# Attention and gated MLP on one core: a new order of the same steps from the 200th step on

## The chip, the core and the metric

The kernel runs on one core of one Trainium2 chip. The metric is device time in microseconds (us). A core has five engines with an instruction queue each: PE (TensorE, the matrix unit), DVE (VectorE), ACT (ScalarE), POOL (GpSimd) and SP (SyncE, which here only issues DMAs). Each works its queue strictly in order: an instruction that waits holds up everything behind it on its engine. Engines wait for one another through semaphores.

## The reference

The computation has two parts, all in fp32, and the output of the first is the input of the second:

```python
# attention, B=8 batches, H=8 heads, S=576, D=64, window 128
scores = q @ k.T / 8;  scores += -slope[h] * |i - j|
scores = where(0 <= i - j < 128, scores, -1e9)
attn = softmax(scores)                       # row maximum taken off first
x = (attn @ v) with the heads side by side   # (8, 576, 512)
# gated MLP
u, v = split(gelu_tanh(x @ w_in), 2)         # 512 + 512 columns
v_n = (v - mean(v)) / sqrt(var(v) + 1e-6) * g_ln
v_s = w_sg @ v_n (over the sequence) + b_sg
out = x + (u * v_s) @ w_out
```

## The kernel before, in words

The work is cut into 2015 named steps. A step is a handful of instructions of one engine: one transpose group, one group of exponentials, one DMA issue. The function `attention_gmlp` defines them all and then builds them in the order of one string, `ORDER` (L1150 to L1232). The loop below it (L1234 to L1250) runs the steps in that order and ties every instruction to the one before it on its engine, so the string fixes the queue of each engine word for word. How the steps of different engines mix in the string also decides which on-chip buffer a step gets: pools hand out buffers in the order of the string (2 banks each of the PSUM pools `ps_s`, `ps_a`, `ps_m`, 1 `px`, 2 `qk`), and a step that takes a buffer waits for the last reader of its earlier content.

The 64 (batch, head) problems are 32 *pairs* n (batch n//4, two heads). The steps of pair n, each a letter and n:

- `q`, `L`: loads of q and k (L250) and of v (L257, L259), issued by SP.
- `a`, `c`, or `*` for both: score matmuls on PE (L278). `A` `B` `C` `G`: bias, mask and row minimum of the negated scores on DVE (L302, L295).
- `e` `E` `f` `F` `j`: exponentials on ACT (L311). `R`: inverse of the row sums on DVE (L322, L323). `r` `s` `S`: scaling by it on POOL (L334).
- `t` `T`: transposes of the two heads on PE (L347) into a bank of `ps_a`; `z` the first block's (L360). `X` `Y`: masked copies of them to the one buffer `px` on DVE (L356). `V`: attn @ v on PE (L384, L388), which reads `px`.
- `p` `x` on ACT and `2` on DVE (L396): the result gathered in SBUF. `h` (L401), `l` (L218), `k`: its split in a high and a low part. fp32 products run as three matmuls of such parts, high x high, high x low, low x high (L607 to L609).

The MLP of batch b has, with b as the digit behind the letters: `w` and `v` (x times the columns of v, 512 wide, L607 to L609), `vg` gelu (ACT L786), `n..`/`vn` the normalization (L725 to L742), `tt` `tj` `tg` the last 64 rows (PE L796 and L798, DVE L802 and L803, ACT L811), `u`/`U` the u columns (PE L607 to L609 for batches 0 and 1, L905 for later ones) with their evacuations `uc`, `ue` (DVE L914), `ut`, `y` the product with w_sg (L607 to L609, L940, L941), `gm` the gate (DVE L946), `gh` (ACT L1006) `gl` (POOL L224) `gt` (DVE L1019) its split, `O` the product with w_out (PE L1059), `oa` (DVE L1066, L1069) and `D` the stores (SP L1081). `Us` `Uh` `Ul` (DVE L649 and L659 among them) add rows of weights once, early in the program, and `lu`, `lo` (SP L686) load such sums again per batch. The early steps `i` `d` `b` `o` `+` `H` `-` load and split the weights (ACT L192, L194, L203; DVE L196, L198, L208). `W` steps are filler matmuls (L1139).

ACT needs another function table for gelu than for exp. Where a gelu step follows an exponential in the order, a one-element gelu is put in ahead (L1237), whose row in the trace is preceded by the load of the table; the way back loads one at the exponential (L311).

Of the kernel before, what the change touches and what calls it, by code (L numbers as in the profile page):

```python
# [21 lines left out]
def attention_gmlp(  # L22
# [1123 lines left out]
    for b in range(B):  # L1146
# [10 lines left out]
        l2 v03 v02 v00 v01 W1 e5 j5 vg03 H10 vg02 vg00 vg01 -5 b9 o9 -7 -4 nv30b nv00b nv10b -10 +9 nv00p u000 u030
        u001 F5 k0 H9 nv10c nv00c -9 E5 nv00h f5 k3 nv30c vn00 L5 i11 q7 i8 wl1 q4 tl R5 a4 u031 A4 B4 s5 t5 nv20b r5
        z5 uc00 wH1 k2 tH uc03 j4 E4 w-1 nv10p S5 nv20p t- e4 nv10h X5 c4 C4 f4 G4 P5 F4 bl L4 wl0 tt0 T5 u020 Y5 R4
        vn01 tj0 s4 r4 u021 V5 t4 nv20c u010 tg0 d11 nt0b nv30p x5 p5 wH0 S4 nt0p w-0 X4 25 T4 z4 u011 Y4 nv20h uc02  # L1160
        nv30h P4 bH nt0c vn03 b- vn02 V4 nt0h x4 d8 p4 uc01 tn0 b11 o11 b8 24 o8 y020 y021 *7 +11 ug0 A7 +8 B7 y000
        y001 H11 j7 H8 Us0 C7 G7 -11 -8 Us1 gm02 gm00 F7 E7 f7 e7 q9 q6 L6 *6 A6 R7 gh00 gh02 h4 B6 C6 e6 q8 L7 s7
        y010 y011 t7 S7 gl02 r7 T7 y030 G6 gm01 X7 F6 E6 f6 j6 R6 gl00 s6 S6 Y7 y031 z7 gm03 gh01 h5 P7 V7 p7 gh03
        gl01 t6 T6 X6 Y6 Oa0 x7 gl03 r6 O00 z6 27 oa00 Us2 l4 l5 P6 h7 V6 p6 x6 Us3 26 O01 h6 l6 l7 *8 oa01 A8 B8 C8
        Us4 G8 u100 u101 e8 *9 E8 f8 j8 F8 R8 A9 B9 u110 s8 S8 r8 t8 C9 k4 k7 Uh1 uc10 E9 j9 f9 e9 k5 k6 Ul1 X8 G9
        u111 T8 Y8 Uh0 z8 Ul0 Us5 F9 uc11 P8 tt1 L9 D00 L8 V8 u130 Us6 R9 s9 tj1 Ud1 S9 t9 u120 Uh2 tg1 X9 Us7 Ul2 Ud2
        Ud0 D01 q10 q11 Us8 Us9 nt1b T9 u131 uc13 x8 28 u121 Y9 nt1c O03 nt1p r9 z9 Uh3 nt1h uc12 P9 Ul3 ks0 ks1 ks2
        V9 p9 x9 p8 oa03 ks3 29 ks4 tn1 kh0 kh1 kl0 O02 ks5 *10 A10 B10 C10 G10 j10 e10 E10 f10 F10 oa02 kl1 v10 *11
        v11 A11 R10 vg10 vg11 B11 nv01b nv01c C11 nv11b r10 s10 nv01p S10 nv11p z10 t10 ug1 v12 nv11c X10 v13 T10 P10
        nv11h vn11 nv01h vn10 vg12 nv21b G11 vg13 nv31b Y10 nv21c nv31c ks6 nv21p h9 l9 nv31p ya100 ya110 ya101 ya111  # L1170
        f11 e11 nv21h nv31h j11 kd0 q12 q13 L10 L11 D03 kd1 D02 V10 vn12 kh2 F11 E11 vn13 y100 y101 y110 y111 ks7 kl2
        gm10 ks8 ks9 R11 kh3 gm11 kl3 y120 y121 s11 t11 y130 gh11 gl11 y131 x10 210 gm12 gt11 p10 h8 gh15 X11 gm13 O11
        S11 gl15 r11 gt12 T11 z11 O15 h10 gh12 gh16 gh13 P11 Y11 oa11 gl12 V11 x11 p11 gl16 gt13 O16 211 gh17 oa15
        oa16 gt14 *13 gl13 O13 gl17 ut25 oa13 O17 A13 oa17 O12 B13 oa12 h11 gh14 gl14 l8 O14 C13 oa14 G13 l10 l11 E13
        k10 uh25 k9 k11 k8 v20 v21 vg20 ul25 vg21 j13 ut26 ut27 nv02b nv02c nv02p nv02h nv12b nv12p nv12c nv12h vn20
        vn21 *12 tt2 U21 kd2 lu21 lu22 q14 lu20 L12 D11 D10 q15 L13 tj2 U25 uh27 f13 uh26 e13 ue21 A12 B12 ut24 ul27
        ul26 U26 F13 ue25 U23 uh24 E12 ue26 U27 C12 ue23 G12 R13 e12 f12 j12 F12 U22 ue27 R12 ul24 U24 ue22 r12 s12
        z12 t12 S12 tg2 nt2b nt2p s13 X12 nt2c ue24 v22 T12 Y12 v23 vg22 nv22b P12 nt2h tn2 vg23 V12 p12 x12 nv32b
        nv32c 212 nv22c nv22p nv32p S13 h12 l12 r13 ug2 nv22h nv32h ya200 ya210 *14 A14 B14 vn22 ya201 t13 ya211 z13
        vn23 y200 y201 X13 gm20 C14 y210 y211 y220 T13 gm21 G14 E14 P13 f14 gh21 j14 F14 e14 Y13 gl21 y221 *15 y230  # L1180
        R14 A15 gt21 B15 gm22 C15 r14 s14 S14 y231 gh25 f15 gm23 gl25 gt23 gt22 z14 t14 V13 E15 gh23 P14 p13 x13 gh27
        O21 gh22 j15 X14 213 lo21 q16 lo22 D13 q17 D12 lo20 L14 L15 T14 O25 G15 Y14 gh26 V14 p14 F15 x14 e15 gl23 gl27
        gl22 oa21 gl26 O26 oa25 O23 ut35 gt24 214 R15 oa26 oa23 *16 A16 B16 C16 O27 s15 S15 r15 z15 t15 h14 k12 gh24
        h13 E16 P15 j16 l13 gl24 l14 G16 oa27 X15 k13 e16 uh35 F16 f16 O22 T15 Y15 O24 *17 R16 oa22 oa24 A17 B17 V15
        s16 r16 S16 x15 p15 215 h15 ul35 l15 C17 f17 e17 t16 X16 T16 G17 ut37 Y16 L16 q19 lu32 D21 lu30 D23 L17 q18
        lu31 D20 v30 z16 k15 k14 j17 P16 F17 E17 tt3 tj3 *18 V16 R17 ut36 tg3 vg30 nt3b nt3c nt3p uh37 x16 ul37 nt3h
        v31 216 nv03b tn3 U31 uh36 vg31 ue31 U35 A18 B18 nv13b ut34 ul36 U36 r17 s17 t17 z17 ue35 uh34 ue36 C18 nv13c
        U33 ue33 X17 S17 nv03p nv13p ul34 U37 U32 ue37 T17 U34 nv13h P17 j18 E18 f18 vn31 ue32 G18 nv03c Y17 nv03h
        ue34 p16 F18 e18 vn30 v33 D22 R18 *19 vg33 V17 x17 ug3 A19 s18 B19 C19 nv33b 217 nv33c v32 t18 ya310 vg32 E19
        nv23b nv23c r18 S18 nv33p nv23p j19 ya300 ya301 z18 ya311 X18 nv23h nv33h p17 vn32 vn33 e19 h17 G19 h16 P18  # L1190
        F19 l17 k17 f19 lo32 L19 L18 lo31 q20 q21 lo30 T18 y310 Y18 y300 y301 *20 gm30 R19 A20 V18 B20 x18 r19 s19 S19
# [79 lines left out]
```

## Time and profile before

| what | value |
|---|---|
| median of 3 runs | 577.96 us (577.95 to 578.33) |
| span of the profiled execution | 577.4 us |
| PE busy | 560.8 us, 97% of the span |
| DVE busy | 473.8 us, 82% |
| ACT busy | 378.6 us, 66% |
| POOL busy | 308.0 us, 53% |
| DMA | 69.78 MB, mean 121 GB/s |

The profiled execution's span is 577.4 us, about half a microsecond under the median of the runs; what the runs count beyond it lies around the span. Busy time is a sum over the whole program; where an engine waits, and for which other, is read from single stretches.

### The profile page before, as it was taken

Reading aid. Unit: us, or ns where it says so; the run is one execution under the profiler, and the core shown is the slowest. Engines: PE = TensorE matmul, PEld = TensorE weight load, DVE = VectorE, ACT = ScalarE, POOL = GpSimd, SP = SyncE. Lnnn points to the kernel's source line nnn. Section 1 sums busy time; section 2 is a strip of 40 time slices with the busy share of each in tenths; the row PEclk is TensorE's granted clock in tenths of the full one; section 3 lists DMA queues with packets and bytes.
Section 4 is the critical chain, followed back from the end, with each engine's and each line's share of the span. In section 5 each row is a group of like instructions: output and inputs, shape, how many; then the busy total and the mean of one; then the engine's idle time right before and its main releaser. Section 6 shows DMA issues by size and latency. Waiting matters only on the chain.

```text
span 577.4 us, 14654 instructions
## 1 busy us (share of the span) xinstructions
PE 560.8 (97%) x5495; PEld 512.7 (89%) x5495; DVE 473.8 (82%) x1324; ACT 378.6 (66%) x1063; POOL 308.0 (53%) x365
## 2 busy tenths in 40 slices
PE   5889999999999999999999999999999999999997
PEld 4667899998899799997999998998989999998997
DVE  7989998799989868899788987878897988666646
ACT  7988997466853867467776576746695667833422
POOL 3676646530436543575447753496347653576325
PEclk9989999999999999999999999999999999999999
DMA  8675213216403413454260465135332606012502
GB/s 297 190 235 199 72 45 121 69 46 243 167 37 125 156 37 99 146 192 129 60 212 10 140 204 173 43 103 168 130 120 65 214 2 197 2 35 96 171 1 82
DMA packets 43561, 69.78 MB, mean 121 GB/s; under 512 B 3554, under 2 KB 31202, under 8 KB 43492
## 3 DMA queue, kind: packets, MB, share of 16 engines
q1 hardware_dynamic: 43492, 68.86, 36.7%
q8 instruction: 43, 0.70, 0.5%
q14 instruction: 26, 0.21, 0.1%
...
## 4 chain that ended last, share of the span: by engine, by line
PE 90%; DVE 5%; DMA 2%; ACT 1%; issue 1%; POOL 0%; SPq 0%; DVEq 0%; ACTq 0%
PE ps_m L607 13%; PE ps_m L1059 13%; PE ps_m L609 12%; PE ps_m L608 12%; PE ps_m L905 12%; PE ps_a L347 5%; PE ps_s L384 4%; PE ps_s L278 4%; PE ps_a L278 4%; PE ps_m L384 3%; DMA qk<-qkT 2%; PE ps_m L941 2%; PE ps_m L940 1%; DVE px L356 1%; DVE e L295 1%; PE ps_m L796 1%
## 5 line engine op out<-in xcount | busy, mean ns | idle before, releaser
L334 POOL TENSOR_TENSOR e<-e,rr 128x256 f32<-128x256 f32 (+2 forms) x116 | 80.7, 718 | 97.0 <-DVE rr L323 84.9
L311 ACT ACTIVATE e<-e,stats 128x128 f32<-128x128 f32 (+1 forms) x288 | 110.6, 386 | 17.7 <-DVE stats L295 17.1
L224 POOL TENSOR_TENSOR region<-u,region 128x288 fp32r<-128x288 f32 (+1 forms) x78 | 77.7, 1016 | 44.7 <-ACT region L1006 16.2
L356 DVE TENSOR_TENSOR px<-ps_a,m_both 128x1024 f32<-128x1024 f32 x64 | 77.4, 1216 | 5.9 <-PE ps_a L347 5.4
L607 PE MATMUL ps_m<-ws,region 128*128 128x288 f32 x256 | 78.2, 306 | 0.0
L609 PE MATMUL ps_m<-ws,region 128*128 128x288 f32 x256 | 75.7, 296 | 0.0
L608 PE MATMUL ps_m<-ws,region 128*128 128x288 f32 x256 | 75.6, 295 | 0.0
L730 POOL TENSOR_TENSOR rs<-rs,mhalf 128x1 f32<-128x1 f32 (+1 forms) x40 | 30.2, 756 | 57.4 <-DVE rs L727 57.2
L218 POOL TENSOR_TENSOR xs<-xf,xs 128x288 fp32r<-128x288 f32 (+1 forms) x48 | 49.9, 1060 | 13.8 <-ACT xs L401 13.8
L311 ACT ACTIVATION_READ_ACCUMULATOR e<-e,stats 128x1 f32 x288 | 54.4, 189 | 0.0
L1006 ACT ACTIVATE region<-u 128x576 fp32r<-128x576 f32 x35 | 23.7, 684 | 43.4 <-PE ps_m L608 17.4
L607 PEld LDWEIGHTS ps_m<-ws,region 128*128 128x128 f32 x256 | 48.3, 189 | 1.5 <-issue 0.8
L608 PEld LDWEIGHTS ps_m<-ws,region 128*128 128x128 f32 x256 | 48.2, 188 | 0.1
L609 PEld LDWEIGHTS ps_m<-ws,region 128*128 128x128 f32 x256 | 48.1, 188 | 0.1
L607 PE MATMUL ps_m<-wi,xs 128*128 128x512 f32 x112 | 46.9, 418 | 0.1
L1066 DVE TENSOR_TENSOR xf<-ps_m,xf 128x576 f32<-128x576 f32 x48 | 35.7, 750 | 10.9 <-PE ps_m L1059 10.1
L609 PE MATMUL ps_m<-wi,xs 128*128 128x512 f32 x112 | 44.3, 395 | 0.0
L608 PE MATMUL ps_m<-wi,xs 128*128 128x512 f32 x112 | 44.2, 395 | 0.0
L946 DVE TENSOR_TENSOR u<-ps_m,u 128x576 f32<-128x576 f32 x32 | 24.0, 752 | 18.7 <-PE ps_m L941 11.5
L347 PE MATMUL ps_a<-ident,e 128*128 128x128 f32 x256 | 38.0, 275 | 1.0 <-DVE px L356 1.0
L295 DVE CUSTOM_DVE_ANT_0 e<-ps_s,bias 128x128 f32<-128x128 f32 (+1 forms) x140 | 34.9, 287 | 2.5
L278 PE MATMUL ps_s<-qk 64*64 64x192 f32 (+2 forms) x576 | 31.5, 333 | 5.3 <-DMA qk<-qkT 4.9
(217 smaller groups left out, 1600.9 us busy)
## 6 DMA issues: line engine op xcount, KB each, us to landing
...
```

The lines of the kernel that those rows point to most:

```text
L218: (engine or nc.gpsimd).tensor_tensor(out[:, cs], a[:, cs], b[:, cs], op)
L224: nc.gpsimd.tensor_tensor(out[:, fs], a[:, fs], b[:, fs], ALU.subtract)
L278: return lambda: nc.tensor.matmul(banks[half][to, c:c + k1 - k0], qk[js, 0, q0:q0 + R], qk[js, 1, k0:k1], start=True, stop=True)
L311: nc.scalar.activation(x, x, AF.Exp, bias=self.nm[0:n, i:i + 1], scale=-1.0, accum_out=self.sm[0:n, i:i + 1])
L334: nc.gpsimd.tensor_tensor(x[:, z:z + step, :], y[:, z:z + step, :], self.rr[0:n, i + z:i + z + min(k, step)].rearrange("p (m o) -> p m o", ...
L347: burst([lambda t=t: nc.tensor.transpose(cv[:, t // 2, t % 2], self.pr[j][:, t, :].rearrange("p (h c) -> p h c", h=2), ident[:, j * R:j * ...
L356: nc.vector.tensor_tensor(xv, cv, mv, ALU.mult)
L607: nc.tensor.matmul(dst, ah, bh, start=(first and i == 0), stop=False)
L608: nc.tensor.matmul(dst, ah, bl, start=False, stop=False)
L609: nc.tensor.matmul(dst, al, bh, start=False, stop=(last and i == n - 1))
L905: nc.tensor.matmul(dst, left(n, g, c)[:, ms], right(n, h, c), start=first and c == 0 and k == 0, stop=c == 1 and k == 2, skip_group_check= ...
L1059: nc.tensor.matmul(dst, p, q, start=first and f == 0 and k == 0, stop=f == 1 and k == 2, skip_group_check=True)
```

## The change

The string `ORDER` is another one from its 200th step on: the same 2015 steps, each once. The first 200 stand as before, about to the steps of pair 2. Nothing else in the program differs; the string has two lines fewer, so that lines behind it have numbers smaller by 2. The number of table loads that the order makes necessary goes from 30 to 32.

```diff
@@ -1150,83 +1150,81 @@
     ORDER = """
...
-        T2 X2 Y2 l3 w31 w11 z2 d4 d10 P2 V2 x2 H7 p2 b4 o4 b10 o10 22 +4 +10 w13 w33 *5 A5 B5 C5 G5 w03 w23 h2 H4 d9
...
+        Y2 l3 w31 w11 z2 d4 d10 P2 V2 x2 H7 p2 b4 o4 b10 o10 22 +4 +10 q6 H4 i11 k0 w23 wl1 k3 w33 L4 w13 d9 -5 b9 -7
+        w03 tl *5 h2 l2 v02 A5 B5 C5 H10 v03 vg02 v00 o9 vg03 vg00 -4 nv00b q4 v01 vg01 e5 G5 nv10b +9 H9 u030 i8 nv00p
...
```

PE, transposes of pair 4: the L347 row is `T4`, the L360 row `z4`, the L607 to L609 rows ahead of it are the end of `u010` (12 matmuls) and those behind it the beginning of `u011`; `t4` is ahead of `u010`. Before:

```order
217 L607 MATMUL ps_m<-xs,wi 128x288
218 L608 MATMUL ps_m<-xs,wi 128x288
219 L609 MATMUL ps_m<-xs,wi 128x288
220 L347 MATMUL ps_a<-ident,e 128x2x64 x4
221 L360 MATMUL ps_a<-ident,e_0_122 128x128
222 L607 MATMUL ps_m<-xs,wi 128x288
223 L608 MATMUL ps_m<-xs,wi 128x288
```

and now, from the last matmul of the product of pair 5 on (L388), `t4` and `T4` as one row of 8:

```order
206 L388 MATMUL ps_a<-p_2_121,vt 64x64
207 L347 MATMUL ps_a<-ident,e 128x2x64 x8
208 L607 MATMUL ps_m<-xs,wi 128x288
209 L608 MATMUL ps_m<-xs,wi 128x288
210 L609 MATMUL ps_m<-xs,wi 128x288
211 L607 MATMUL ps_m<-xs,wi 128x288
212 L608 MATMUL ps_m<-xs,wi 128x288
```

`T4` was behind `u010` and stands directly behind `t4` now; both u groups come behind it.

DVE, from the second minima group of pair 6 to the masked copies `X7` and `Y7` (the L356 rows). The L946 rows are the gate of batch 0, L322 and L323 are `R6`. Before:

```order
278 L302 COPY_PREDICATED ps_s<-sel,ps_s 128x2x64
279 L295 ISA e,stats_126<-ps_s,bias_103 128x128
280 L295 ISA stats_126 128x1
281 L295 ISA e,stats_126<-ps_s,bias_103 128x128
282 L295 ISA stats_126 128x1
283 L946 TENSOR_TENSOR u<-ps_m,u 128x576
284 L356 TENSOR_TENSOR px<-ps_a,m_both 128x4x256
285 L322 TENSOR_SCALAR rr<-stats_126 128x9
286 L323 RECIPROCAL rr<-rr 128x9
287 L356 TENSOR_TENSOR px<-ps_a,m_both 128x4x256
288 L946 TENSOR_TENSOR u<-ps_m,u 128x576
```

and now:

```order
278 L946 TENSOR_TENSOR u<-ps_m,u 128x576
279 L659 TENSOR_TENSOR sum<-sums,sum 128x512
280 L302 COPY_PREDICATED ps_s<-sel,ps_s 128x2x64
281 L295 ISA e,stats_126<-ps_s,bias_103 128x128
282 L295 ISA stats_126 128x1
283 L295 ISA e,stats_126<-ps_s,bias_103 128x128
284 L295 ISA stats_126 128x1
285 L946 TENSOR_TENSOR u<-ps_m,u 128x576
286 L322 TENSOR_SCALAR rr<-stats_126 128x9
287 L323 RECIPROCAL rr<-rr 128x9
288 L356 TENSOR_TENSOR px<-ps_a,m_both 128x4x256 x2
289 L649 TENSOR_TENSOR sums<-sums,wi 128x512
```

`R6` stands ahead of both masked copies and no longer between them, and `Ul0` (L659) has come ahead of them; further up, one more of the sums of weights (`Us2`, L649) is ahead too.

DVE at the minima of pair 5 (L302 and the rows behind it; `xf_134` is the gather of pair 2). Before:

```order
142 L396 TENSOR_TENSOR xf_134<-ps_s,xf_134 128x512
143 L302 COPY_PREDICATED ps_a<-sel,ps_a 128x2x64
144 L295 ISA e,stats_130<-ps_a,bias_101 128x128
145 L295 ISA stats_130 128x1
146 L295 ISA e,stats_130<-ps_a,bias_101 128x128
147 L295 ISA stats_130 128x1
148 L295 ISA e_1_124,stats_130<-ps_a,bias_101 128x64
```

and now:

```order
142 L396 TENSOR_TENSOR xf_134<-ps_s,xf_134 128x512
143 L208 TENSOR_TENSOR wi<-tmp,wi 128x512
144 L196 TENSOR_SCALAR tmp<-tmp 128x512
145 L208 TENSOR_TENSOR wi<-tmp,wi 128x512
146 L302 COPY_PREDICATED ps_a<-sel,ps_a 128x2x64
147 L295 ISA e,stats_130<-ps_a,bias_101 128x128
148 L295 ISA stats_130 128x1
```

Three weight instructions, which stood behind the minima of pair 5, are ahead of them now. On PE the scores `*5`, for which the first L302 row waits, have moved behind two more groups `w` of three 512-column matmuls.

Four moves of single steps later in the program: on SP the load `q18` stands behind `lu31` and ahead of the stores `D20` to `D22`, where it was behind `lu32`, `lu30`, two stores and `L17`; on DVE `tj3` is directly behind `R17`, where it was ahead of it; on PE `T12` is directly behind `t12`, where `v22` was between them; on DVE `gm62` is ahead of `Y31`, where it was behind it.

## Rows read from the trace of the kernel before

**Rows 1.** The page: busy time of each engine, and the clock in 40 slices.

```profile
PE 560.8 (97%) x5495; PEld 512.7 (89%) x5495; DVE 473.8 (82%) x1324; ACT 378.6 (66%) x1063; POOL 308.0 (53%) x365
...
PEclk9989999999999999999999999999999999999999
```

**Rows 2.** All waits of PE, grouped: waiting line, releaser, total us, times, longest.

```profile
PE ps_m L905 <- PE ps_m L905: 0.9, 1, 0.9
PE ps_a L278 <- DMA qk<-qkT: 0.8, 1, 0.8
...
PE ps_m L607 <- ACT xf L786: 0.4, 1, 0.4
```

**Rows 3.** Busy time of each engine in three stretches of 14.4 us, and the clock.

```profile
57.60:72.00 14.40, 14.40 (x129) 12.68 (x131) 13.88 (x46) 13.48 (x45) 9.80 (x12) 1.00 0.24 69
72.00:86.40 14.40, 14.40 (x188) 13.42 (x181) 13.84 (x31) 13.80 (x24) 7.22 (x7) 1.00 0.15 46
86.40:100.80 14.40, 14.40 (x162) 13.60 (x161) 12.00 (x45) 10.30 (x43) 9.37 (x9) 1.00 0.39 123
```

**Rows 4.** DVE in time at pair 5: start, length, line, operation, [idle before <-releaser].

```profile
49.73 0.68 DVE L396 TENSOR_TENSOR xf<-ps_s,xf 128x512 f32<-128x512 f32 x1
51.06 0.29 DVE L302 COPY_PREDICATED ps_a<-sel,ps_a 128x128 f32<-128x128 uint8 x1 [0.65 <-PE ps_a L278]
```

**Rows 5.** DVE by line and shape: count, busy us, mean ns.

```profile
L196 DVE TENSOR_SCALAR tmp<-tmp 128x512 int32<-128x512 int32 x12 | 5.7, 487 | 0.0
L208 DVE TENSOR_TENSOR wo<-tmp,wo 128x512 fp32r<-128x512 f32 x2 | 1.4, 686 | 0.0
L649 DVE TENSOR_TENSOR sums<-wi 128x512 f32<-128x512 f32 x4 | 2.7, 685 | 0.0
L659 DVE TENSOR_TENSOR sum<-sums,sum 128x512 fp32r<-128x512 f32 x6 | 4.2, 706 | 0.0
L1019 DVE TENSOR_TENSOR u<-u 128x576 f32<-128x576 f32 x28 | 25.9, 937 | 5.8 <-POOL spare L224 5.2 <-POOL region L224 0.2
```

**Rows 6.** PE in time at the first u products.

```profile
55.16 0.39 PE L607 MATMUL ps_m<-wi,xs 128*128 128x512 f32 x1
...
55.85 0.69 PE L1139 MATMUL ps_a<-spare 128*128 128x288 f32 x4
56.98 0.40 PE L607 MATMUL ps_m<-xs,wi 128*128 128x288 f32 x1 [0.43 <-ACT xf L786]
```

**Rows 7.** PE in time at the transposes of pair 4.

```profile
73.41 0.66 PE L347 MATMUL ps_a<-ident,e 128*128 128x128 f32 x4
73.82 0.38 PE L607 MATMUL ps_m<-xs,wi 128*128 128x288 f32 x1
...
75.50 0.60 PE L347 MATMUL ps_a<-ident,e 128*128 128x128 f32 x4
```

**Rows 8.** POOL in time at the same place.

```profile
73.55 1.04 POOL L334 TENSOR_TENSOR e<-e,rr 128x512 f32<-128x512 f32 x1
```

**Rows 9.** DVE in time at the masked copies of pair 7.

```profile
94.98 1.22 DVE L356 TENSOR_TENSOR px<-ps_a,m_both 128x1024 f32<-128x1024 f32 x1
96.96 0.51 DVE L322 TENSOR_SCALAR rr<-stats 128x9 f32<-128x9 f32 x1 [0.76 <-ACT e L311]
97.63 1.16 DVE L356 TENSOR_TENSOR px<-ps_a,m_both 128x1024 f32<-128x1024 f32 x1
```

**Rows 10.** PE in time at the product of pair 7 with v.

```profile
98.91 1.40 PE L384 MATMUL ps_s<-px,vt 64*64 64x128 f32 x29
```

**Rows 11.** All engines in time at the scores of pair 18.

```profile
263.97 0.69 DVE L802 COPY vg<-ps_m 64x512 f32<-64x512 f32 x1 [0.40 <-PE ps_m L798]
264.70 0.68 DVE L803 TENSOR_TENSOR vg<-ps_m,vg 64x512 f32<-64x512 f32 x1
264.74 0.88 PE L278 MATMUL ps_a<-qk 64*64 64x128 f32 x20 [0.81 <-DMA qk<-qkT]
265.31 0.15 DVE L322 TENSOR_SCALAR rr<-stats 128x9 f32<-128x9 f32 x1
```

**Rows 12.** The chain of work that ended last, in time: start, us, what.

```profile
259.54 5.07 DMA qk<-qkT
```

**Rows 13.** POOL in time at pair 12.

```profile
207.28 2.40 POOL L334 TENSOR_TENSOR e<-e,rr 128x128 f32<-128x128 f32 x3 [3.34 <-DVE rr L323]
```

**Rows 14.** PE in time at the same place.

```profile
208.97 0.60 PE L347 MATMUL ps_a<-ident,e 128*128 128x128 f32 x4
```

**Rows 15.** PE in time at the first product with w_out of batch 6.

```profile
509.66 0.30 PE L941 MATMUL ps_m<-wsB,vB 66*128 66x288 f32 x1
510.00 0.77 PE L1059 MATMUL ps_m<-fifth,wo 128*128 128x288 f32 x4
```

**Rows 16.** ACT by line and shape: table loads.

```profile
L1237 ACT ACT_TABLE_LOAD x15 | 19.2, 1283 | 0.2
```

More of the change, by code (lines that the diff above doesn't have):

```diff
@@ L1157, in attention_gmlp @@
[L1157 to L1191, printed above, removed]
@@ new lines, in attention_gmlp @@
+        tg0 wl0 nv20c nv30p V5 p5 bl t4 wH0 uc02 r4 x5 nv30h S4 T4 nt0b X4 Y4 u010 u011 d8 nv20h 25 w-0 bH nt0c nt0p z4
+        P4 vn02 V4 nt0h b- vn03 tn0 y020 x4 uc01 b11 24 p4 o11 b8 *7 o8 +8 A7 B7 y021 ug0 e7 C7 G7 H8 +11 y000 f7 H11 -8
+        gm02 E7 q9 -11 Us0 F7 y001 Us1 Us2 j7 *6 R7 gh02 gl02 s7 Uh0 S7 A6 B6 C6 e6 y010 y011 gm00 L6 t7 h4 T7 E6 f6
+        y030 gh00 y031 gl00 r7 j6 Ul0 G6 F6 L7 gm01 R6 s6 X7 Y7 gh01 gl01 S6 z7 P7 V7 r6 p7 t6 T6 Us3 gm03 gh03 gl03 Us4
+        Uh1 h5 Us5 X6 Y6 x7 l5 Oa0 27 O00 h7 l7 Us6 z6 Ul1 P6 V6 l4 p6 q8 x6 Uh2 26 h6 oa00 O01 Us7 l6 k6 oa01 D01 *8 A8
@@ new lines, in attention_gmlp @@
+        oa12 F13 ut27 ut26 uh26 v20 ut24 oa14 D12 vg20 nv02b nv02c nv02p v21 R13 s13 r13 vg21 nv12b nv12c tt2 U21 nv12p
+        *12 nv02h nv12h L12 vn20 uh27 vn21 tj2 ue21 A12 B12 C12 G12 j12 ul27 lu21 ul26 e12 U25 ue25 f12 U26 ue26 U23
+        ue23 U27 lo22 E12 uh24 ul24 ue27 F12 R12 r12 U22 D10 s12 S12 ue22 tg2 nt2b nt2c U24 t12 nt2p X12 T12 q14 v22
+        ue24 ug2 nt2h vg22 Y12 v23 nv22b nv22c nv22p z12 z13 P12 V12 tn2 nv22h ya210 vn22 vg23 x12 L14 nv32b nv32p 212
+        p12 h12 nv32c nv32h l12 vn23 ya211 P13 ya200 ya201 *14 A14 e14 j14 y210 y211 B14 C14 S13 G14 gm21 y200 y201 E14
@@ new lines, in attention_gmlp @@
+        T16 h15 G17 l15 v30 f17 uh36 F17 oa22 k15 tt3 X16 Y16 D20 E17 e17 ul36 ut37 uh37 R17 r17 tj3 *18 D21 q19 lu30
+        vg30 tg3 s17 A18 B18 nt3b nt3c nt3p V16 x16 S17 216 v31 t17 nt3h ul37 tn3 U31 vg31 nv13b ut34 ue31 C18 nv13p
+        nv03b nv03c U35 ue35 lu32 uh34 q20 U36 U33 lo32 nv03p p16 ue36 U37 G18 z17 F18 ue33 ul34 U32 X17 j18 L17 ue37
+        U34 T17 nv13c e18 ue32 nv03h vn30 L18 lo30 nv13h vn31 f18 v33 E18 R18 lo31 r18 s18 P17 ue34 ug3 Y17 vg33 *19 V17
+        p17 S18 x17 A19 B19 v32 nv33b nv33c nv33p 217 ya310 nv33h C19 G19 t18 T18 ya311 vg32 nv23b nv23c f19 X18 nv23p
@@ new lines, in attention_gmlp @@
+        gm61 gh61 gl61 gt61 k28 y620 y621 y630 gm62 T31 Y31 y631 gh65 gl65 O61 gm63 gh63 gt63 gt62 O65 gh62 oa61 gh67
+        gh66 gl63 lu70 gl67 z31 gl66 P31 gl62 V31 x31 O66 lu71 k29 oa65 O63 231 oa66 O67 p31 ut75 h31 l31 k31 tt7 oa63
+        O62 gt64 gh64 oa67 gl64 O64 v70 uh75 ul75 tj7 tg7 nt7b ut77 uh77 ut76 uh76 lu72 ul76 v71 ut74 nt7c nt7p oa62
+        nt7h oa64 U71 ul77 U75 vg70 nv07b nv07c nv07p ue71 U76 uh74 ul74 ue75 tn7 U73 lo72 vg71 ue76 nv07h lo71 nv17b
+        nv17p U77 ue73 U72 nv17c nv17h ue77 U74 ue74 D63 v72 ue72 ug7 v73 vn71 vn70 ya710 ya700 vg72 nv27b nv27p nv27c
```

94 lines of the change are left out of this document (53 added, 41 removed).

## The prediction, made before the changed kernel was run

> **What bounds the kernel now.** I read the page first. [...] The list of PE's waits comes second. In the part that is re-ordered it names three above 0.3 us: 0.9 in the U products of batch 2 (behind products on PE's own results), 0.8 on the load of pair 18, and 0.4 on a gelu [rows 2]. Third, the busy time by stretches: from 57.6 to 86.4 us DVE is busy for 13.9 and 13.8 of 14.4 us, from 86.4 on for 12.0, while PE shows no gap [rows 3]. In this stretch two engines are full at once. A step of DVE that is put ahead of what PE needs shows as a wait of PE there, whereas elsewhere DVE has time to catch up. The timelines of the single places, the fourth view, give the terms below.
>
> The arithmetic is the same in number and size, so no term comes from the work itself. The chain that ended last is PE's, so a wait that PE loses or gets moves the end by its length, as long as nothing later swallows it.
>
> **First place: pair 5, 50 to 57 us.** A5 started at 51.06 after an idle time of 0.65 [rows 4]. Now three weight instructions stand ahead of it: one of 0.49 and two of about 0.69, some 1.7 us with their small overlap [rows 5]. The scores on which A5 waits are behind two more groups of three 512-column matmuls, 0.69 us each by the start of the fillers behind such a group (55.85 - 55.16) [rows 6]. The scores come at 51.06 + 1.38 = 52.4, DVE is free at 50.4 + 1.7 = 52.1, so A5 starts at about 52.5, with 1.7 us of later work already done: level with before (51.06 + 1.7 = 52.8), since the idle time is filled. PE gains something here: the first u product waited 0.43 for a gelu [rows 6], and now the gelus stand ahead of the exponentials of pair 5 on ACT, so this wait goes. But h2, the split of pair 2, has gone behind four other ACT steps, and the low part that POOL makes from it is wanted by v02's third matmul on the other side. I put that wait at 0.4 too, since it is the same 1.2 us of weight split on ACT and the same idle time of PE in front. Taken: 0; bounds -0.43 (no wait for the low part) and +0.5.
>
> **Second place: T4, 74 us.** Before, PE reached T4 at 75.50, after u010. Now T4 follows t4 directly. t4 starts at 73.41 and the next began at 73.82 [rows 7], so T4 is reached at 73.85. It reads what S4 scales on POOL, and S4 ran from 73.55 for 1.04, to 74.59 [rows 8]. POOL's and DVE's work ahead of S4 and R4 is the same in sum in both orders, and DVE is full here [rows 3], so S4 has no reason to come sooner. PE waits 74.59 - 73.85 = 0.74. u010, which covered this, now comes after. Bounds: 0 (if R4 comes 0.7 sooner) and +1.0 (if POOL is later by a scaling's fraction).
>
> **Third place: Y7 and V7, 95 to 99 us.** V7 started at 98.91 [rows 10], a tenth behind the end of Y7, which ran from 97.63 for 1.16 [rows 9]; so PE is level with DVE here and any lateness of DVE is PE's. Ahead of Y7 there are now two more instructions, Us2 of 0.69 and Ul0 of 0.71 [rows 5], 1.4 us in all. Against them stands the idle time of 0.76 in front of R6 [rows 9], and that R6 itself (0.6) has moved ahead of both copies, where it still has to wait for the last exponentials of pair 6. I take the 1.4 less the 0.76, so Y7 ends about 0.65 late, bounds 0 and +1.4. The waits at T4 and at V7 don't add: what PE has lost at T4 it no longer waits at V7. The later of the two counts, 0.75, with bounds 0 and +1.5.
>
> [...]
>
> **Fourth place: the load of pair 18, 264 us.** The scores *18 waited 0.81 us for a load [rows 11] that was issued at 259.54 and took 5.07 [rows 12], behind stores and another load in SP's queue. Now it is ahead of them, so this wait goes. What is late next is V16: its bank of PSUM is freed by tj3, whose two instructions started at 263.97 and 264.70 [rows 11]. In the new order R17 (0.15 and 0.21) is ahead of tj3, and R17 waits for exponentials until 264.0; tj3 ends at about 265.8 instead of 265.4. PE would reach V16 at 265.5 and wait 0.4. Net: -0.4; bounds -0.81 and 0.
>
> **Two small ones.** At batch 6 the first product with w_out started 0.2 us late (510.00, where 509.66 + 0.13 was the pace) [rows 15], because the gate gm62 ran behind a masked copy; now it is ahead of it: -0.2, bounds -0.25 and 0. At pair 12, T12 follows t12 directly. POOL's three scalings of the pair ran from 207.28 for 2.40, to 209.68 [rows 13]; PE began t12 at 208.97 [rows 14], so it would reach T12 at about 209.3 and wait 0.4, less the 0.2 by which R12, with one inverse fewer ahead of it, is sooner: +0.2, bounds 0 and +0.5.
>
> **What I cost at nothing.** The wait of 0.9 in batch 2 [rows 2] stays, since the steps ahead of it are the same. Two more changes of ACT's table cost 1.28 us each on ACT [rows 16], which is busy for 66% of the span [rows 1]; the idle third hides them, and if they fall where PE waits for a gelu they cost up to 2.6 us together. [...] The end of the program keeps its chain, and the stores that moved to it find SP free. The hundreds of other moves shift waits that are under 0.3 us each; I take them as even, and put +-0.8 us on them, the size of the largest single wait that the list shows [rows 2].
>
> **The sum.** 0 + 0.75 - 0.4 - 0.2 + 0.2 = +0.35 us. On the profiled span of 577.4 that is 577.8; the median of the runs stands half a microsecond above this span, 577.96, and goes to 578.3. The bounds of the terms, added up, are -1.7 and +3.75; all ends at once are unlikely.
>
> **The rivals.**
>
> Faster: DVE's queue isn't late in the full stretch. R4 and S4 come sooner, so that T4 is met without a wait, and R6's idle time takes in all of Us2 and Ul0. Then only the removed waits count: 0.43 at the first u product, 0.81 at *18 and 0.2 at the w_out product [rows 6, 11, 15], -1.4 us in all, and 576.5. For it speaks that each of these waits has one clear releaser that moved ahead. Against it speaks that DVE has only 0.5 us of idle time in each 14.4 us between 57.6 and 86.4 [rows 3], so that R4 can't come much sooner, and that *18 has a second wait right behind it.
>
> Slower: the full stretch loses what it lends. [...] The sum is 1.5 + 0.4 - 0.2 = +1.7, so 579.6. It decides from where Y7 ends 1.4 us late, that is beyond 100.2 in the trace. For it speaks that V7 started a tenth behind Y7 already [rows 9, 10]; against it the 0.76 of idle time there.
>
> Table changes on the path: one or two of the extra loads fall in front of a gelu that PE waits for, as the one in the first u product did [rows 6]. Each adds 1.28 less what idle time is there; with the forecast's sum the end is at 579.6 to 580.9. Against it: ACT is idle for a third of the time.
>
> That the new order is in effect the old one, with no difference beyond the chance of a run, is part of the forecast's case, since its sum is so small.
>
> **How the numbers follow.** A difference under 0.2% (1.16 us) can't be told from none in a measurement of this kernel. So faster means under 576.8 and slower over 579.1. The forecast, in which gains and losses cancel to within that, has a chance of 0.43; its own range is 577.0 to 579.0. The faster rival has 0.29. The slower one has 0.20, and the table changes 0.08. That is faster 0.29, same 0.43, slower 0.28. The predicted time is the forecast's, 578.3. For 8 times in 10 the range leaves a tenth at either side: it reaches from 575.9, half a microsecond below the faster rival (the small moves at work on its side), to 580.2, half a microsecond above the slower.
>
> **What would show it.** In the trace after: PE's first u product without a wait for a gelu, and instead a wait of some 0.4 in v02; an idle time of some 0.7 us ahead of T4, released by POOL; Y7 ending 0.6 to 0.8 later than PE's pace, and V7 right behind it; the scores *18 without a wait for a load, with V16 waiting 0.4 for tj3; and the first product with w_out of batch 6 on pace. The forecast is wrong if PE shows no wait at T4 or V7 (then faster), or if DVE is behind PE by over 1.4 us at V7, or if a wait of over 1 us appears that none of these places has (then slower).

## The result, and the profile after

The changed kernel takes 584.74 us (584.68 to 585.09, 4 runs) against 577.98 for the one before (577.95 to 578.33, 4 runs): the ratio is 1.0116, 95% interval 1.0102 to 1.0131. It is 6.8 us slower; the forecast was +0.35, and the range ended at 580.2.

The page of the changed kernel, its span, the busy times and the clock, beside [rows 1]:

```profile
span 583.4 us, 14672 instructions
...
PE 561.5 (96%) x5495; PEld 511.3 (88%) x5495; DVE 478.9 (82%) x1324; ACT 384.2 (66%) x1066; POOL 314.4 (54%) x365
...
PEclk9999999999999999999999999999999999999999
```

PE does the same work in the same time (561.5 against 560.8), but the span has grown by 6 us: PE waits more. The second thing to see is on DVE and POOL. They run the same instructions as before, 1324 and 365, and are busy for 5.1 and 6.4 us more. Instructions got longer, not more.

The profiled execution of before was itself one with a low clock, 0.88 in the stretch from 28.8 to 43.2 us. Later runs of the same kernel had spans of 575.9 to 577.5, most near 576.2, and nearly all took 1.7 to 1.9 us more than their span. So the half microsecond that I took as lying outside was wrong, and the two traces are compared from V2 on (46.9 and 46.3 us), behind that stretch. The starts of a few steps on PE, read from both traces:

| step on PE | before, us | after, us | stretch behind the row above: after less before |
|---|---|---|---|
| V2 | 46.88 | 46.31 | |
| V6 | 104.84 | 107.16 | +2.89 |
| V12 | 215.51 | 219.31 | +1.48 |
| V17 | 286.92 | 291.92 | +1.20 |
| V24 | 399.35 | 405.15 | +0.80 |
| last matmul | 573.57 | 579.09 | -0.28 |
| end of span | 577.4 | 583.4 | +0.4 |

The sum is 6.5 us. Five sixths of it are lost by 292 us, and the largest piece before 107 us.

The row of V17 is too small by 0.6. From V12 to V17 the trace of before takes 71.4 us, but the four later traces that have its order in this stretch (e2, e8, e11, e12) take 70.8. The difference is the wait of the scores *18 for their load. In before's trace the load took 5.07 us [rows 12] and PE sat idle for 0.81 [rows 11]; in e8, e11 and e12 it took 4.4 to 4.5. PE in e8:

```profile
264.21 0.60 PE L278 MATMUL ps_a<-qk 64*64 64x128 f32 x10 [0.22 <-DMA qk<-qkT]
```

In e2, e11 and e12 the same row has no idle time ahead of it. Most of this wait belonged to one execution. Against the other four, the new order loses 1.8 us from V12 to V17, and 7.1 in all.

The waits of PE in the changed kernel that the list names from 0.4 us up, and that stand where the order is new, beside [rows 2] (waiting line, releaser, total, times, longest):

```profile
PE ps_a L347 <- POOL e L334: 1.1, 2, 0.6
PE ps_m L905 <- PE ps_s L278: 1.0, 1, 1.0
PE ps_m L607 <- ACT vg L786: 1.0, 1, 1.0
...
PE ps_m L905 <- ACT vg L786: 0.9, 1, 0.9
PE ps_m L1059 <- DVE xf L1066: 0.7, 1, 0.7
PE ps_m L384 <- PE ps_s L278: 0.6, 1, 0.6
PE ps_m L609 <- POOL xs L218: 0.5, 1, 0.5
...
PE ps_a L347 <- ACT p L363: 0.4, 1, 0.4
```

Eight lines where before had three, and six different releasers. By the semaphores that the waiting instructions carry, they are, in order of time: v02 on l2, v01 on vg00, t5 on s5 and T4 on S4 (the first line's two), O17 on oa16, U25 on tj2 (as before), T16 on P16, V16 on tj3 (the list names PE here, a releaser inferred wrongly), and U35 on vg31.

Where DVE takes its extra time, the whole stretch from V2 to V7 in the kernel before and after (length, then busy time and count of PE, PEld, DVE, ACT, POOL):

```profile
46.88:98.91 52.03, 51.59 (x536) 46.16 (x535) 48.62 (x153) 45.97 (x129) 30.89 (x30) 1.00 0.36 115
```

```profile
46.31:100.75 54.44, 51.90 (x536) 45.95 (x536) 50.79 (x154) 46.17 (x129) 31.75 (x30) 1.00 0.33 101
```

The stretch is 2.41 us longer and DVE is busy for 2.17 us more of it. Of that, 1.4 are the two sums Us2 and Ul0, which the prediction had. One gate of 0.75 (gm03), which stood ahead of V7 before, has left the stretch. The instructions that both orders have in it are some 1.5 us longer in sum: R7 by 1.2 and an L208 by 0.9, which both began beside POOL, and smaller differences of either sign. DVE in the changed kernel, at two places:

```profile
49.76 1.58 DVE L208 TENSOR_TENSOR wi<-tmp,wi 128x512 fp32r<-128x512 f32 x1
...
91.50 1.39 DVE L322 TENSOR_SCALAR rr<-stats 128x9 f32<-128x9 f32 x1
```

and POOL there:

```profile
49.47 1.33 POOL L218 TENSOR_TENSOR tmp<-tmp,wst 128x512 int32<-128x512 int32 x1 [0.78 <-DVE tmp L198]
51.59 1.98 POOL L218 TENSOR_TENSOR xs<-xf,xs 128x576 fp32r<-128x576 f32 x1 [0.80 <-ACT xs L401]
...
91.17 1.68 POOL L218 TENSOR_TENSOR region<-u,region 128x576 fp32r<-128x576 f32 x1 [2.07 <-ACT region L950]
```

The L208 of step -5, one of the three weight instructions that moved ahead of A5, takes 1.58 us instead of 0.69 [rows 5]; POOL's instruction began 0.3 us before it and ended at 50.80. R7, an addition on 128x9 numbers that takes 0.17 us elsewhere, takes 1.39 and ends within 0.05 us of POOL's L218. And l2 on POOL takes 1.98, where most other splits of this size take up to 1.46: DVE's next L208 ran beside it, from 51.60 for its usual 0.68.

### The profile page after: what moved, and what is told of

Read it like the earlier page. It is cut to its first block, busy times and chain, and to the rows that moved or that the text cites. A ratio compares the mean times of both kernels' runs of the same rounds, so it can differ in the third digit from the quotient of the medians.

```text
span 583.4 us, 14672 instructions
## 1 busy us (share of the span) xinstructions
PE 561.5 (96%) x5495; PEld 511.3 (88%) x5495; DVE 478.9 (82%) x1324; ACT 384.2 (66%) x1066; POOL 314.4 (54%) x365
## 4 chain that ended last, share of the span: by engine, by line
PE 82%; DVE 9%; ACT 4%; issue 2%; DMA 1%; POOL 1%; SPq 0%; DVEq 0%; POOLq 0%; ACTq 0%
PE ps_m L1059 12%; PE ps_m L607 12%; PE ps_m L905 11%; PE ps_m L609 11%; PE ps_m L608 11%; PE ps_a L347 4%; PE ps_s L384 3%; PE ps_a L278 3%; PE ps_m L384 3%; PE ps_s L278 3%; DVE px L356 2%; DVE e L295 2%; ACT e L311 2%; PE ps_m L941 1%; PE ps_m L940 1%
## 5 line engine op out<-in xcount | busy, mean ns | idle before, releaser
L356 DVE TENSOR_TENSOR px<-ps_a,m_both 128x1024 f32<-128x1024 f32 x64 | 76.5, 1214 | 3.4 <-PE ps_a L347 3.3
L607 PE MATMUL ps_m<-ws,region 128*128 128x288 f32 x256 | 78.0, 305 | 0.0
L609 PE MATMUL ps_m<-ws,region 128*128 128x288 f32 x256 | 75.5, 295 | 0.0
L730 POOL TENSOR_TENSOR rs<-rs,mhalf 128x1 f32<-128x1 f32 (+1 forms) x40 | 33.2, 830 | 77.6 <-DVE rs L727 77.4
L218 POOL TENSOR_TENSOR xs<-xf,xs 128x288 fp32r<-128x288 f32 (+1 forms) x48 | 53.6, 1134 | 16.7 <-ACT xs L401 16.7
L607 PEld LDWEIGHTS ps_m<-ws,region 128*128 128x128 f32 x256 | 48.2, 188 | 1.7 <-issue 1.1
L609 PEld LDWEIGHTS ps_m<-ws,region 128*128 128x128 f32 x256 | 48.1, 188 | 0.0
L607 PE MATMUL ps_m<-wi,xs 128*128 128x512 f32 x112 | 46.5, 415 | 1.0 <-ACT vg L786 1.0
L609 PE MATMUL ps_m<-wi,xs 128*128 128x512 f32 x112 | 44.3, 396 | 0.5 <-POOL xs L218 0.5
L725 DVE BATCH_NORM_STATS2 st<-vg 128x6 f32<-128x512 f32 (+1 forms) x38 | 26.2, 690 | 19.4 <-ACT vg L786 17.4
L347 PE MATMUL ps_a<-ident,e 128*128 128x128 f32 x256 | 37.6, 276 | 2.6 <-POOL e L334 1.1
L1066 DVE TENSOR_TENSOR xf<-ps_m,xf 128x576 f32<-128x576 f32 x48 | 35.8, 750 | 2.6 <-PE ps_m L1059 2.3
L1059 PE MATMUL ps_m<-region,sum 128*128 128x288 f32 x252 | 36.9, 299 | 0.2 <-ACT xf L366 0.2
```

The source lines that it names most:

```text
L218: (engine or nc.gpsimd).tensor_tensor(out[:, cs], a[:, cs], b[:, cs], op)
L347: burst([lambda t=t: nc.tensor.transpose(cv[:, t // 2, t % 2], self.pr[j][:, t, :].rearrange("p (h c) -> p h c", h=2), ident[:, j * R:j * ...
L356: nc.vector.tensor_tensor(xv, cv, mv, ALU.mult)
L607: nc.tensor.matmul(dst, ah, bh, start=(first and i == 0), stop=False)
L609: nc.tensor.matmul(dst, al, bh, start=False, stop=(last and i == n - 1))
L1059: nc.tensor.matmul(dst, p, q, start=first and f == 0 and k == 0, stop=f == 1 and k == 2, skip_group_check=True)
```

## The experiments

All kernels are the order of before or of after with a few steps moved in the string; nothing else differs. Ratios are to the kernel before, timed on the same chip. "Waits" are the places of PE as above; their lengths are counted from start to start on PE, less the usual pace of such a pair of matmuls, and so are 0.1 to 0.4 us longer than the idle time in the list.

**e1 and e2: which half of the order loses.** One order up to V6, the steps that are left in the other's order.

```diff
 e1: order of before up to V6, then the remaining steps in the order of after
 e2: order of after up to V6, then the remaining steps in the order of before
```

> The order of before up to V6 (about 107 us), then the order of after for all other steps. Theory A (the time is lost at separate places where PE waits, each with its own releaser, and the waits up to V6 sum to 2.9 us more than before): 584.7 - 2.9 = 581.8 us, and the later waits (O17 0.9, T16 0.6, V16 0.7, U35 1.0) are there as in after. Rival B (one early delay of DVE and POOL is carried through the program, so that the later waits are its echo): the later waits go too, 578 to 579 us.

> The order of after up to V6, then the order of before. Theory A: only the early waits (l2, vg00, s5, S4, Y7) are left, 578.0 + 2.9 = 580.9 us. Rival B: the delay is carried on and makes waits in the old order as well, 583 to 585 us.

e2 took 581.08 us, ratio 1.0049 (1.0032 to 1.0066): +2.9, as theory A has it, with the early waits to within 0.02 us of those in after and no others. e1 took 584.32, 1.0104 (1.0088 to 1.0119), which hit neither number. Its trace tells why: the waits at O17, T12, T16, V16, U35 and U25 are those of after to within 0.03 us, so the late losses are no echo of the early ones; but at the junction *8 and u100 wait for steps of pair 6 that the two orders have at different places, and from V6 to V12 the trace is 2.4 us longer than that of after. From V12 to V24 it loses the same as after, to within 0.1 us. It shows theory A's mechanism; the total is spoilt by the junction.

**e3: a wait that comes from the string and no queue.** v01 writes the PSUM tile that vg00 reads. In after it stands behind vg00 in the string.

```diff
-v00 o9 vg03 vg00 -4 nv00b q4 v01 vg01
+v00 v01 o9 vg03 vg00 -4 nv00b q4 vg01
```

> The order of after with v01 directly behind v00 in the string; the queue of every engine is the same word for word, only the place of v01 against vg02, vg03 and vg00 on ACT changes. Theory A: v01 waited 1.1 us for vg00 because it writes the tile that vg00 reads and stands behind it in the string; now vg00 waits for v01 instead, the wait of PE is gone and the time falls by 0.9 to 1.1 us, to 583.7. Rival (DVE is full from 50 to 100 us, so PE's gain comes back as longer waits at t5, T4 and V7): the wait at v01 goes, those three grow by as much, the time stays within 0.3 us of 584.7.

585.13 us, 1.0115 (1.0100 to 1.0130). The wait of 1.1 at v01 is gone, and t5's has grown from 0.7 to 1.6. The rival is right: the wait was real, and without it the runs are no faster (in the trace the stretch from V2 to V6 is 0.35 us shorter).

**e4: POOL's ul37 away from tn3.** In after tn3 on DVE began during one POOL instruction and lasted until the next had ended. DVE, and then POOL, in after:

```profile
274.54 2.15 DVE L742 SCALAR_TENSOR_TENSOR vA<-vg,rs,vA 64x512 fp32r<-64x512 f32 x1 [0.60 <-ACT vA L738]
```

```profile
273.72 1.03 POOL L334 TENSOR_TENSOR e<-e,rr 128x512 f32<-128x512 f32 x1
274.72 1.41 POOL L224 TENSOR_TENSOR region<-u,region 128x576 fp32r<-128x576 f32 x1
```

```diff
-S17 216 v31 t17 nt3h ul37 tn3 U31 vg31 nv13b ut34 ue31 C18 nv13p nv03b nv03c U35
+S17 216 v31 t17 nt3h tn3 U31 vg31 nv13b ut34 ue31 C18 nv13p nv03b nv03c U35 ul37
```

> The order of after with the POOL step ul37 one step later on POOL (behind nv13p); the other engines' queues are the same. Theory P (tn3 on DVE took 2.15 us instead of 0.75 because it was blocked while POOL ran S17 and ul37, and U35 waited 1.0 us for the gelu behind it): tn3 takes under 1.1 us, U35 waits at most 0.2 us, and the time falls by about 0.8 to 583.9. Rival (tn3 is long for a reason of its own, or another wait takes the place): tn3 still takes about 2 us, or U35 waits still, 584.5 to 584.9 us.

DVE and ACT in e4:

```profile
274.30 0.76 DVE L742 SCALAR_TENSOR_TENSOR vA<-vg,rs,vA 64x512 fp32r<-64x512 f32 x1 [0.60 <-ACT vA L738]
```

```profile
279.41 0.64 ACT L912 COPY u<-ps_m 128x576 f32<-128x576 f32 x1 [2.39 <-POOL region L224]
```

The first half of theory P holds exactly: without POOL's second instruction behind it, tn3 takes 0.76 us and U35 waits no more. The second half fails: the moved ul37 is late for the next evacuation on ACT, U33 waits 0.7 us for that, and the time is 584.59, 1.0110 (1.0095 to 1.0125), 0.15 less than after.

**e5 and e6: repairs of after.** e5 takes e5 and j5 back ahead of the gelus; e6 adds four repairs elsewhere.

```diff
 e5, with v01 as in e3:
-H10 v03 vg02 ... vg01 e5 G5 nv10b +9 H9 u030 i8 nv00p j5
+H10 v03 e5 j5 vg02 ... vg01 G5 nv10b +9 H9 u030 i8 nv00p
 e6, as e5 and: ut25 behind oa16; tj3 ahead of R17; z16 P16 behind B17; D61 behind lu72, D60 behind D62
```

> The order of after with v01 behind v00 (as in e3) and the exponentials e5 and j5 ahead of the table load for the gelus, where ACT idled 1.3 us. Theory A (the head's loss is a chain through ACT: e5 and j5, 1.2 us, were moved behind the gelus, so that F5, R5, s5 and t5 came late, and all that follows R5 on DVE with them): t5's wait of 1.6 us in e3 falls to under 0.7, and the time falls by about 0.8 us against e3's 585.1, to 584.3. Rival (DVE is full there and R5 waits for DVE's own queue): t5's wait stays over 1.2 us and the time at 585.

> e5's order with four more edits at separate places of after: ut25 behind oa16 (O17 waited 0.9 us for oa16, ahead of which ut25 took 1.96 us on DVE beside a POOL step); tj3 ahead of R17 (V16 waited 0.7 for tj3); z16 and P16 ahead of x15 (T16 waited 0.6 for P16, which stood behind x15 and k14 on ACT); the stores D61 and D60 back ahead of the last batch's loads (the end came 0.5 us later behind PE's last matmul). Theory A (places are independent): O17 -0.9, V16 -0.4, T16 -0.5, end -0.4, head -0.8, so 581.7 us. Rival (each wait that goes is taken by the next one, as U35's by U33's in e4): at least half of it stays, 583 us or more.

584.68 (1.0118, 1.0104 to 1.0132) and 584.95 (1.0120, 1.0107 to 1.0134): both rivals. In e5 t5's wait falls from 1.6 to 1.2, but u030 waits 0.5 for vg03, which now comes behind the exponentials. In e6 O17's wait goes and O12 waits 0.5; T16's falls from 0.6 to 0.2, and v30 behind it, which waits for h15 and l15 of pair 15, waits 1.2; U35's wait grows from 1.0 to 1.4. Only the stores did what was expected: from the last matmul's start to the end of the span it is 3.9 us, against 4.3 in after and 3.9 in before.

**e7 and e8: single parts in before.** e7 makes the change's two gains alone, e8 the T4 move alone.

```diff
 e7: q18 and q19 exchanged; gm62 ahead of Y31
 e8:
-t4 nv20c u010 tg0 d11 nt0b nv30p x5 p5 wH0 S4 nt0p w-0 X4 25 T4 z4 u011
+t4 nv20c tg0 d11 nt0b nv30p x5 p5 wH0 S4 nt0p w-0 X4 25 T4 u010 z4 u011
```

> The order of before with two single moves: q18 and q19 change places (q18 then takes the buffer that comes free first, four DMAs earlier in SP's queue), and gm62 ahead of Y31 on DVE. Theory A: the wait of 0.8 us at *18 goes, since tj3 is ahead of R17 here V16 waits 0.2 to 0.4 for it, and O61's 0.2 goes: -0.5 to -0.8, 577.2 to 577.5 us against 578.0. Rival (V16 takes back all): 577.7 to 578.0.

> The order of before with u010 behind T4, so that T4 follows t4 directly; no other queue changes. My prediction's term: PE waits 0.74 us for S4, and y020's wait of 0.27 and V7's level with DVE take some of it back, so +0.4 to +0.75, 578.4 to 578.8 us. Rival (DVE sets V7, so that a wait of PE at T4 is slack): the wait at T4 is there, +0.0 to +0.2 us at the end.

e7: 577.57 us, 0.9995 (0.9986 to 1.0003). *18 no longer waits, V16 waits 0.26 for tj3, O61's wait is gone, and a new one of 0.4 stands at O25. It ends with the load lo20, which was issued at 232.88, 16 us ahead of both exchanged loads: it belongs to this execution and not to the edit. Beside the 0.2 to 0.3 that *18 waits in e2, e8, e11 and e12, V16's 0.26 takes all of that gain back, as the rival says; only O61's 0.2 is left. The sign of the result fits, but the interval includes no change. e8: 579.06 us, 1.0018 (1.0009 to 1.0028), +1.1. PE in e8:

```profile
72.66 0.66 PE L347 MATMUL ps_a<-ident,e 128*128 128x128 f32 x4
74.10 0.63 PE L347 MATMUL ps_a<-ident,e 128*128 128x128 f32 x4 [0.79 <-ACT xf L366]
```

T4 waits, for S4 (ends at 73.84) and p5 (73.96; it ended last), and the stretch from V2 to V6 is 0.8 us longer than in before. The rival, that DVE's pace makes this slack, falls.

**e9 and e10: undo the early moves on DVE.** e9 puts the three weight instructions back behind the minima of pair 5, e10 also the two sums behind Y7.

```diff
 e9, with v01 as in e3:
-w13 d9 -5 b9 -7 w03 tl *5 h2 l2 v02 A5 B5 C5 H10 v03 vg02 v00 o9
+w13 d9 w03 tl *5 h2 l2 v02 A5 B5 C5 -5 b9 H10 v03 vg02 v00 v01 o9 -7
 e10, as e9 and: Us2 Uh0 Ul0 behind Y7
```

> The order of after with v01 behind v00 (as e3) and the three weight instructions (two L208, one L196) back behind the minima A5, B5, C5 on DVE; the queues of PE, ACT and POOL are those of after. [...] Rival (a wait that goes is taken by the next, as in e5): v02's wait goes, the sum of PE's waits up to V7 stays within 0.3 us, 585 us.

> e9 with Us2, Uh0 and Ul0 behind Y7 (Us2 and Ul0 are 1.4 us of DVE ahead of Y7 in after). Theory A (DVE is full up to Y7, and PE's waits at V7 and V6, 0.6 and 0.2 us, are those sums): both waits go, -0.7 us against e9. Rival (R6's exponentials or POOL hold Y7): V7's wait stays over 0.4 us, and the time within 0.3 us of e9's.

Both are slower than after: 585.96 (1.0129, 1.0116 to 1.0142) and 588.46 (1.0177, 1.0164 to 1.0190). In e9 v02's wait falls from 0.8 to 0.2, but t5 waits 1.9 for s5. Behind that wait TensorE's granted clock is about half: from 67.6 to 70.3 us it is 0.51, and the matmuls of u020 follow each other after 0.24 us instead of 0.13. The stretch from t5 to V5, first in e3, whose queue of PE is the same, and then in e9:

```profile
65.41:72.59 7.18, 7.18 (x58) 6.00 (x58) 6.77 (x23) 7.15 (x25) 6.24 (x7) 1.00 0.37 126
```

```profile
65.76:74.44 8.68, 8.68 (x57) 7.23 (x57) 7.39 (x24) 7.34 (x25) 6.71 (x8) 0.80 0.31 104
```

PE is busy throughout in both, and at a granted clock of 0.80 against 1.00 the stretch is 1.5 us longer. Without these 1.5 us the stretch from V2 to V6 would be some 0.2 us shorter than in e3 and 0.6 shorter than in after (an estimate from these rows). The four executions of e9 took 584.20, 585.65, 586.28 and 586.41, with a mean clock of 1.000 in the first and 0.997 in the others: the first is 0.9 us below e3's median of 585.13. So e9 doesn't show that the moves back cost time by themselves.

In e10 V7 and V6 no longer wait, as theory A said, and then this stands on PE:

```profile
101.58 0.66 PE L347 MATMUL ps_a<-ident,e 128*128 128x128 f32 x4
104.51 0.98 PE L347 MATMUL ps_a<-ident,e 128*128 128x128 f32 x4 [2.28 <-POOL e L334]
```

T6 waits 2.3 us for S6: two of the sums that now run there meet POOL (Us4 and Us5 take 1.2 and 1.4 us), and S6 itself takes 1.5, as in after. Here too the clock falls behind the wait (0.50 from 105.2 to 108.0 us): from T6 to V6 it is 5.43 us, against 3.82 in after, so that 1.6 us of e10's loss are the clock's. I had expected the gains and missed what the moved steps would meet in their new place.

**e11 and e12: make the early moves alone, in before.**

```diff
 e11:
-22 +4 +10 w13 w33 *5 A5 B5 C5 G5 w03 w23 ... vg01 -5 b9 o9 -7
+22 -5 -7 +4 +10 w13 w33 *5 A5 B5 C5 G5 w03 w23 ... vg01 b9 o9
 e12: Us2 Us3 from just ahead of V6 and just behind it to behind Us1 (ahead of A6)
```

> The order of before with two of the three weight instructions (L208, steps -5 and -7) ahead of A5 on DVE; the other engines' queues are the same. My prediction's first term says level (0), since 0.65 us of idle time takes them. Theory P: they take up to 0.9 us longer beside POOL, A5 comes 0.7 to 1.5 us late, e5, the table load and the gelus on ACT with it, and the wait at u000 of 0.6 us grows by as much: +0.5 to +1.0 us, 578.5 to 579.0. Rival (level): within 0.2 us of 577.9.

> The order of before with Us2 and Us3 (two L649, 0.69 us each) ahead of A6 on DVE, where after has Us2 and Ul0 (1.4 us) ahead of Y7. My prediction's term: 1.4 less the 0.76 us of idle time ahead of R6, V7 waits about 0.65 us, 578.6. Theory P (DVE is full and POOL may block one of them or R7 by up to 1.2 us): +0.8 to +1.5 us, 578.8 to 579.5. Rival (the idle time takes all): within 0.2 us.

e11: 580.23 us, 1.0042 (1.0027 to 1.0057), +2.1. Its six executions lie in two groups, 579.3 to 579.7 and 580.8 to 582.1; the trace is of the slowest of the first group (579.70) and shows +1.6 from V2 to V6. What the second group met in addition no trace shows. DVE, POOL and PE in e11:

```profile
49.73 3.41 DVE L208 TENSOR_TENSOR wi<-tmp,wi 128x512 fp32r<-128x512 f32 x2
53.06 0.28 DVE L302 COPY_PREDICATED ps_a<-sel,ps_a 128x128 f32<-128x128 uint8 x1
```

```profile
49.44 1.29 POOL L218 TENSOR_TENSOR tmp<-tmp,wst 128x512 int32<-128x512 int32 x1 [0.78 <-DVE tmp L198]
50.70 1.89 POOL L218 TENSOR_TENSOR xs<-xf,xs 128x576 fp32r<-128x576 f32 x1
52.54 1.76 POOL L218 TENSOR_TENSOR wi<-tmp,wi 128x512 fp32r<-128x512 f32 x1
```

```profile
57.98 0.40 PE L607 MATMUL ps_m<-xs,wi 128*128 128x288 f32 x1 [2.03 <-ACT xf L786]
```

Two instructions of 0.69 us [rows 5] take 3.41 between them, and two of the three POOL instructions beside them are 0.5 us longer too. A5 starts at 53.06, 6.8 us behind V2 instead of 4.2, and the exponential, the table load and the gelu behind it hand that to PE: the wait that was 0.43 [rows 6] is 2.03. e12: 579.48 us, 1.0023 (1.0015 to 1.0032), +1.3. No instruction is longer there; DVE's queue is. PE in e12:

```profile
90.77 0.40 PE L607 MATMUL ps_m<-ws,region 128*128 128x288 f32 x1 [1.27 <-DVE u L946]
```

The 1.4 us of sums come out as 1.3 us of wait, not at V7 but seven microseconds sooner, at a PSUM tile that a gate has to free.

**e13 and e14: do the rest's losses stand alone, and can the good end be had?**

```diff
 e13: order of after up to V17, then the remaining steps in the order of before
 e14: order of e7 up to V23, then the remaining steps in the order of after, D61 behind lu72 and D60 behind D62
```

> The order of after up to V17 (about 292 us), then the order of before. Theory A (the losses are local and add: up to V6 2.9 us, from V6 to V12 1.5, from V12 to V17 1.2 in the trace of after): 578.1 + 5.6 = 583.7 us, less what the junction changes. Rival (the later losses depend on the steps that follow, or are made good by the old order): 581 to 582.5 us.

> The order of e7 (before with q18 and q19 exchanged and gm62 ahead of Y31) up to V23, then the order of after with the stores D61 and D60 back ahead of the last batch's loads. Theory A (in the traces after is 0.3 us shorter than before from V24 to the last matmul, and its end 0.5 us longer by the two stores): -0.3 from e7, -0.3 from the last part, the stores at no cost, 577.3 to 577.6 us, a kernel ahead of both. Rival (the junction and V24's neighbourhood take it back): 577.9 or more.

e13: 584.27 us, 1.0109 (1.0094 to 1.0125), +6.5 against the 577.79 of before beside it, a little above theory A's 583.7: in its trace V17 comes 5.5 us later behind V2 than in before, and all that follows takes as long as in before. With the 0.6 by which before's own trace was long from V12 to V17, theory A's figure would have been 584.3. The losses stand alone and add. e14: 581.56, 1.0060 (1.0047 to 1.0072): its junction makes z24 wait 2.6 us for r24, and behind that wait the granted clock falls again (0.50 from 385.3 to 388.6 us), which costs another 1.2 us up to V24. From V24 to the last matmul it takes 173.9 us, as after does, against 174.2 in before, and 3.9 behind that. The 0.3 us exist, but e7 has nearly all of them (174.0): they are mostly O61's wait. This way of joining costs ten times as much. No version that I ran is clearly faster than before.

## Why the prediction was wrong, by its steps

**What bounds the kernel: right, and not taken to its end.** It named the stretch from 57.6 to 86.4 us, where two engines are full, as the place where a step put ahead shows as a wait of PE. The largest loss, 2.9 us up to V6, is there and just ahead of it (e2). But the terms were made as if each DVE instruction kept its length. The bounds were also added up wrongly: those of the five terms give -1.5 and +2.5, and with the +-0.8 for the other moves -2.3 and +3.3, where the prediction has -1.7 and +3.75. The measured +6.8 is outside all of them.

**First place, cost 0: the step that failed first.** The waits there are 0.8 at v02, 1.1 at v01 and 0.7 at t5, less the 0.6 (0.43 in the list) that the first u product waited before: some +2.0 us, where the bound was +0.5. The start of A5 was nearly right: it comes 5.9 us behind V2, and the forecast 52.5 is 5.6. Three other parts were not. First, "level with before" took the weight instructions at their usual lengths. e11 has the move alone in before's order, with two of the three: they took 3.41 us instead of 1.4, with POOL running beside them, and the delay went through A5, e5, the table load and the gelus to PE. In after one of them takes 1.58 us instead of 0.69, and l2 on POOL 1.98 beside the next, over half a microsecond more than most splits of its size; so v02 waits twice the 0.4 that I gave it, and 0.2 in e9, where the weight instructions are back. Second, v01 now waits for vg00, whose tile it takes; this wait was not in the term. Third, that the gelus stand ahead of the exponentials of pair 5 was counted as a gain only. e5 starts 13.1 us behind V2 instead of 5.9, and s5, which t5 waits for, follows from it. e3 and e5 took single waits of these away, and others grew: in e3 t5's by 0.9, in e5 a new one at u030 by 0.5. How the 2.0 us divide among the three causes was not shown.

**Second place, T4, +0.74: right.** In after T4 waits 0.6 us for S4; alone in before (e8) it costs 0.8 us in the trace and 1.1 in the runs, though p5 ended 0.1 us behind S4 there. That it and V7's lateness don't add was wrong in part: in after V7 waits another 0.6.

**Third place, Y7, +0.65: the mechanism right, the size half.** The sums alone cost 1.3 us (e12): DVE had no slack to take them, and the 0.76 of idle time ahead of R6 was not free for work that stands earlier in the queue. R7's 1.2 us beside POOL came on top in after, for which the prediction has no term.

That a DVE instruction gets longer beside POOL is seen in after in the first place too (-5's L208, with both inputs in SBUF, took 1.58 us instead of 0.69 [rows 5]), and behind V6 at ut25 (1.96 us), tn3 (2.15) and two more steps (1.35 to 1.40).

**Fourth place, *18, -0.4: the gain was hardly there.** The wait for the load went, and V16 waited for tj3 as said, but for 0.7 us, not 0.4. The 0.81 on which the term rests was mostly of the one execution that I read: in e2, e8, e11 and e12 *18 waits 0.2 to 0.3. Against those the term is +0.4 and not -0.4; a second trace of before would have shown it. U35 behind it waited 1.0 more for vg31, because tn3 took 2.15 us, 1.4 more than in e4, and T16 ahead of it 0.6 for P16, which had come to stand behind x15 and k14 on ACT. None of these two was in the sum.

**The two small ones: right.** T12 waits 0.2, and O61's wait is gone.

**"The hundreds of other moves ... I take them as even", +-0.8: wrong, by some 3 us.** From V6 on the waits at O17 (0.9; ut25 took 1.96 us beside a split on POOL), T16 and U35 are all losses; O36 and O46, 0.3 each, stand behind splits on DVE (L1019, L1015) that took 1.35 to 1.40 us; that these caused the two waits was not tried. Also in this class: in the new order seven more products V follow a transpose directly, and such a step costs 0.20 us from start to start, where a 288-column group follows a transpose in 0.03. With the other boundaries counted in the same way, from the kinds' typical gaps in both traces, that is +0.7 us for the program, an estimate that no run tests. I had counted it as nothing.

**The end, 0: wrong by 0.4.** D60 and D61 were said to find SP free. SP was, but D61's transfer now stands among the last stores (issued at 575.66, behind D70): with the two moved back (e6) the end is 0.4 us shorter. The two more table loads cost nothing that a wait shows, as forecast.

The slower rival had the right stretch and the right engine, priced at +1.7. No run shows the 1.5 from which its sum starts: the two sums alone cost 1.3 us (e12), R7 took 1.2 us longer beside POOL in after, and V7 waited 0.6 there. Five more places of this kind were missing. What stays open: the losses behind V17 (0.8 us) stand in every trace that has the new order there (e1, for one), but no run took them away; and the traces give 7.1 us where the runs give 6.8.
